# The product of W_v and T: both halves of T in one 256-column matmul, taken from two PSUM banks

## The chip, the cores and the metric

The kernel runs on one core of a Trainium2 chip. The metric is device time in microseconds (us), the median of several runs. The engines are named as the profile names them: PE is TensorE (matmuls; PEld is its weight load), DVE is VectorE, ACT is ScalarE, POOL is GpSimd, SP issues most DMAs.

## The reference, cut to what matters

One transformer block on x of 2048 tokens by 512 features, all in fp32: an adaptive layer norm, linear attention with 32 heads of 16 features, then a bilinear gated unit.

```python
h = layernorm(x) * (1 + ca) + sa
q, k, v = split(h @ wqkv)                            # 512 columns each
pq, pk = phi(q), phi(k)                              # phi(t) = (t+1 if t>0 else exp(t)) + 1e-6
kv  = einsum("bhsd,bhse->bhde", pk, v)               # 16 x 16 per head
den = einsum("bhqd,bhd->bhq", pq, pk.sum(s)) + 1e-6
x = x + ga * ((einsum("bhqd,bhde->bhqe", pq, kv) / den) @ wo)
h = layernorm(x) * (1 + cb) + sb
x = x + gb * (((h @ w_gate) * (h @ w_up)) @ w_down)
```

## The kernel before, in words

Every fp32 operand X of a matmul is held as two tiles of a rounded type, a high part Xh (X copied to that type, on ACT) and a low part Xl = X − Xh (on DVE). A product of two such pairs is three matmuls that add up in PSUM: ah·bh, ah·bl, al·bh. `product` (L215–221) does this with a moving operand of 512 columns.

No v is ever computed for the tokens. A loop over the 16 tiles of 128 tokens adds up T = x̂ᵀ·phi(k), 512 by 512, in the four accumulators `tacc[k]` (`t_tile`), while it projects k of later tiles. After the loop T is scaled by 1 + ca, gets sa times the sum over phi(k) (`zb`), and is split in high and low (`tt_high`, `tt_low`, L780–787). Then `kv_part` (L789–796) multiplies W_vᵀ by T. Only the four 128 by 128 blocks on the diagonal are wanted, since heads of 16 features do not reach beyond them: for each 128-row slice k of W_v and T, and each block g, three matmuls of 128 columns go to the columns g·128 to g·128+127 of one PSUM bank, `kvps`. That makes 4 · 4 · 3 = 48 matmuls.

The bank is then multiplied by the 0/1 mask of the heads (L818, DVE) into `kvf`, and split (L820: ACT L206 for the high part, DVE L207 for the low). `w_full` (L764–772) multiplies each block of the pair `kvp` by a slice of wo and DVE scales the result by ga (L770): this is the folded output weight, which `y_step` applies to phi(q) of each token tile.

The code is in the order in which instructions are issued; no scheduler moves them. Each engine works through its own instructions in that order and waits by semaphore for the others. Around the change, q of tiles 6 to 11 is projected between the steps: `proj` is twelve matmuls of 512 columns (L219, L220, L221, four times) into a bank of the pool `ps_w`; `q_a` is two ACT instructions on it (L327, L328); `q_b` is one DVE instruction (L331) that reads the bank for the last time. `ps_w` has four banks and `ps_acc` four; a new bank waits for the last reader of the tile that held it. `den_a` is DVE work on the denominators (L712, L718). The piece in question runs, in the program's order: projection 7; `kv_part(0, 1)`; `q_b(6)`, `q_b(7)`; projection 8; `den_a`; `kv_part(2, 3)`; mask and split; `q_a(8)`; projection 9; `q_b(8)`; `w_out(0, 1)`, which is `w_full` and a split; `q_b(9)`; projection 10; `w_full(2, 3)`; projection 11.

The line numbers above are those of the kernel before. In the changed kernel the halves of T are split on L792 and L796, the matmuls are L805 and L806, and the result is taken on L812 to L815.

Of the kernel before, what the change touches and what calls it, by code (L numbers as in the profile page):

```python
# [9 lines left out]
F32R = mybir.dt.float32r  # L10
AF = mybir.ActivationFunctionType
ALU = mybir.AluOpType
AX = mybir.AxisListType

P = 128
# [7 lines left out]
def tile_adaln_block(  # L23
# [12 lines left out]
    nc = tc.nc  # L36
    ctx.enter_context(tc.manual_schedule())
    _, S, D = x.shape
    F = w_gate.shape[1]
    KD = D // P  # L40
# [21 lines left out]
    ps_acc = pool("ps_acc", 4, space=bass.MemoryType.PSUM)  # L62
    ps_w = pool("ps_w", 4, space=bass.MemoryType.PSUM)

    def f32(ap):
        return ap.bitcast(F32)
# [3 lines left out]
    def T(p, tag, shape=(P, D), dt=F32, bufs=None):  # L70
        cnt[0] += 1
        return p.tile(list(shape), dt, tag="t" if p is tiles else tag, name=f"{tag}_{cnt[0]}", bufs=bufs)

    def B(tag, shape=(P, D), dt=F32):

        return T(tiles, tag, shape, dt)

    def acc_bank():
        return T(ps_acc, "acc")

    def bank():
        return T(ps_w, "bank")
# [7 lines left out]
    mask = consts.tile([P, P], F32, name="mask")  # L90
# [114 lines left out]
    def split(src, h, l, low=None):  # L205
        nc.scalar.activation(h, src, AF.Copy)  # L206
        (low or nc.vector).tensor_tensor(l, src, f32(h), op=ALU.subtract)  # L207
# [7 lines left out]
    def product(ps, pairs, begin=True, end=True):  # L215

        n = len(pairs)
        for i, ((ah, al), (bh, bl)) in enumerate(pairs):
            nc.tensor.matmul(ps, ah, bh, start=begin and i == 0, stop=False)  # L219
            nc.tensor.matmul(ps, ah, bl, start=False, stop=False)  # L220
            nc.tensor.matmul(ps, al, bh, start=False, stop=end and i == n - 1)  # L221
# [13 lines left out]
    def cut(pair, a, b):  # L235
        return pair[0][:, a:b], pair[1][:, a:b]
# [78 lines left out]
    wk, wq, wv = [], [], []  # L315
    kx, phk, phq, q_ps = {}, {}, {}, {}

    def proj(i, w, of=bank):

        ch, j = divmod(i, NJ)  # L320
        ps = of()
        product(ps, [(cut(norm[ch].t[k], j * P, (j + 1) * P), w[k]) for k in range(KD)])
        return ps
# [52 lines left out]
    def q_a(i, ps):  # L376
        phq[i] = B("h")
        q_ps[i] = ps
        phi_a(ps, phq[i])

    def q_b(i):
        phi_b(q_ps.pop(i), phq[i])
# [193 lines left out]
    raw_m, raw_o, wo_s = {}, [], []  # L576
# [143 lines left out]
    def den_a(ch, *js, on=None):  # L720

        for j in js:
            den_p(ch, j, on=on)
            den_r(ch, j)
# [25 lines left out]
    def q_tile(i):  # L750
        q_a(i, proj(i, wq))
# [3 lines left out]
    def w_out(*gs):  # L755
        fs = w_full(*gs)
        for f in fs:
            w_split(f)
# [5 lines left out]
    def w_full(*gs):  # L764
        fs = []
        for g in gs:
            ps = bank()
            product(ps, [(cut(kvp, g * P, (g + 1) * P), wo_s[g])])
            f = B("n")
            nc.vector.tensor_tensor(f, ps, ga, op=ALU.mult)  # L770
            fs.append(f)
        return fs
# [4 lines left out]
    ps = proj(6, wq)  # L777
    fs, tt = [], []

    def tt_high(k):  # L780
        f = fs[k]
        nc.vector.scalar_tensor_tensor(f, zb, sa[:, k:k + 1], f, op0=ALU.mult, op1=ALU.add)
        tt.append((B("w", dt=F32R), B("w", dt=F32R)))
        nc.scalar.activation(tt[k][0], f, AF.Copy)

    def tt_low(k):
        nc.vector.tensor_tensor(tt[k][1], fs[k], f32(tt[k][0]), op=ALU.subtract)

    def kv_part(*ks):  # L789
        for k in ks:  # L790
            for g in range(KD):
                a, b = g * P, (g + 1) * P  # L792
                (ah, al), (bh, bl) = cut(wv[k], a, b), cut(tt[k], a, b)
                for n, (x, y) in enumerate(((ah, bh), (ah, bl), (al, bh))):
                    nc.tensor.matmul(kvps[:, a:b], x, y, start=k + g + n == 0, stop=k == KD - 1 and n == 2,
                                     skip_group_check=True)  # L796

    for k in range(KD):
        fs.append(B("n"))
# [1 line left out]
    for k in range(KD):  # L801
        tt_high(k)
        if k:
            tt_low(k - 1)
    tt_low(KD - 1)  # L805
    q_a(6, ps)  # L806
    q_tile(7)
    kvps = acc_bank()
    kv_part(0, 1)
    q_b(6)  # L810
    q_b(7)
    den_p(1, 2)  # L812
    ps = proj(8, wq)
    den_a(0, 2, 3, on=nc.vector)
    kv_part(2, 3)  # L815
    kvp = (B("xh", dt=F32R), B("xl", dt=F32R))
    kvf = B("n")
    nc.vector.tensor_tensor(kvf.rearrange("p (g c) -> p g c", g=KD), kvps.rearrange("p (g c) -> p g c", g=KD),  # L818
                            mask.unsqueeze(1).to_broadcast([P, KD, P]), op=ALU.mult)
    split(kvf, *kvp)  # L820
    q_a(8, ps)
    ps = proj(9, wq)
    q_b(8)
# [4 lines left out]
    ps = proj(10, wq)  # L828
    den_c(0)
    q_a(10, ps)  # L830
    wf = w_full(2, 3)
    den_c(1)
    ps = bank()
# [607 lines left out]
    for n, (s, g, f) in enumerate(order):  # L1441
        groups = groups_of[s]
        first, final = f == groups[g][0], f == groups[g][-1]
# [8 lines left out]
        at = {p: list(early.get((n, p), ())) for p in ("a11", "s1", "s2", "s3", "mid", "s4", "pe")}  # L1452
# [39 lines left out]
        if (s, f) in pair_of:  # L1492
            at_first = f == groups[g][0]
            p = pairs.setdefault((s, g), Pair())
# [20 lines left out]
        if was and was[:2] in paired and was[2] == groups_of[was[0]][was[1]][1]:  # L1515
            of, p = was[0], pairs[was[:2]]
# [87 lines left out]
```

## Time and profile before

| | |
|---|---|
| median of 3 runs | 553.78 us (553.54, 553.78, 557.78) |
| span of the profiled execution, first to last instruction | 552.4 us |
| median less the span | 1.4 us |
| mean granted TensorE clock | 0.999 |
| PE busy | 545.8 us (99%) |
| DVE busy | 432.2 us (78%); 26.07 of 28 us from 152 to 180 us |
| ACT busy | 299.5 us (54%) |
| POOL busy | 176.8 us (32%) |
| the 48 matmuls of L795 | 132.7 to 141.2 us of the span, in two pieces of 24 |

Times within the span are counted from its first instruction. A row of the timeline gives the start, how long it took, engine, line, what it wrote and read with the shape of its tile, and in brackets how long the engine had been idle and what ended that. Instructions of one engine overlap at their ends, so the distance from one start to the next is shorter than a duration; where the two differ, the text says which is meant.

### The profile page before, as it was taken

Reading aid. Unit: us, or ns where it says so; the run is one execution under the profiler, and the core shown is the slowest. Engines: PE = TensorE matmul, PEld = TensorE weight load, DVE = VectorE, ACT = ScalarE, POOL = GpSimd, SP = SyncE. Lnnn points to the kernel's source line nnn. Section 1 sums busy time; section 2 is a strip of 40 time slices with the busy share of each in tenths; the row PEclk is TensorE's granted clock in tenths of the full one; section 3 lists DMA queues with packets and bytes.
Section 4 is the critical chain, followed back from the end, with each engine's and each line's share of the span. In section 5 each row is a group of like instructions: output and inputs, shape, how many; then the busy total and the mean of one; then the engine's idle time right before and its main releaser. Section 6 shows DMA issues by size and latency. Waiting matters only on the chain. (4 is left out here: it accounts for less than half of the span.)

```text
span 552.4 us, 8146 instructions
## 1 busy us (share of the span) xinstructions
PE 545.8 (99%) x2775; PEld 460.1 (83%) x2775; DVE 432.2 (78%) x794; ACT 299.5 (54%) x535; POOL 176.8 (32%) x180
## 2 busy tenths in 40 slices
PE   8999999999999999999999999999999999999997
PEld 6888888888888888888888888878888888888886
DVE  6878779978998998865655767797577877879696
ACT  4876857456467876654545355463243534453540
POOL 2000000003527646353556644540002524242400
PEclk9999999999999999999999999999999999999999
DMA  8910224203230045195888634289786534342004
GB/s 256 373 57 1 76 77 152 77 0 77 78 115 2 0 154 189 39 316 180 285 286 274 222 123 163 87 312 391 231 259 218 173 131 138 129 146 86 1 0 153
DMA packets 58512, 83.24 MB, mean 151 GB/s; under 512 B 6564, under 2 KB 23720, under 8 KB 58472
## 3 DMA queue, kind: packets, MB, share of 16 engines
q1 hardware_dynamic: 56544, 81.16, 44.1%
q10 hardware_dynamic: 1928, 1.58, 0.9%
q8 instruction: 22, 0.36, 0.3%
q14 instruction: 18, 0.15, 0.1%
HBM read 53.02 MB, written 29.69 MB: 150 GB/s over the span
## 5 line engine op out<-in xcount | busy, mean ns | idle before, releaser
L1057 PE MATMUL bank<-h,w 128*128 128x512 f32 (+1 forms) x924 | 221.6, 391 | 0.2 <-POOL w L1020 0.2
L1057 PEld LDWEIGHTS bank<-h,w 128*128 128x128 f32 (+1 forms) x924 | 168.2, 186 | 36.2 <-POOL w L1020 0.6
L1063 ACT ACTIVATE bank<-bank 128x512 f32<-128x512 f32 (+2 forms) x46 | 26.2, 571 | 122.7 <-PE bank L1057 122.5
L1253 DVE TENSOR_TENSOR x<-acc,x 128x256 f32<-128x256 f32 x132 | 48.0, 414 | 13.7 <-PE acc L1226 13.1
L1226 PE MATMUL acc<-w,kh 128*128 128x256 f32 x308 | 57.1, 282 | 0.0
L1226 PEld LDWEIGHTS acc<-w,kh 128*128 128x128 f32 x308 | 50.6, 190 | 3.7
L1020 POOL TENSOR_TENSOR w<-raw,w 128x256 fp32r<-128x256 f32 (+3 forms) x22 | 24.7, 1121 | 73.7 <-ACT w L1013 64.1
L219 PE MATMUL bank<-w,h 128*128 128x512 f32 x112 | 44.1, 394 | 0.0
L221 PE MATMUL bank<-w,h 128*128 128x512 f32 x112 | 43.7, 390 | 0.0
L220 PE MATMUL bank<-w,h 128*128 128x512 f32 x112 | 43.6, 390 | 0.0
L1226 PE MATMUL acc<-w,kl 128*128 128x256 f32 x154 | 43.5, 283 | 0.0
L871 PE MATMUL acc<-w,xh 128*128 128x512 f32 x128 | 40.7, 399 | 0.0
L712 POOL TENSOR_TENSOR f<-h,zb 128x512 f32<-128x512 f32 x12 | 17.5, 1468 | 62.9 <-ACT zb L692 48.9
L262 POOL TENSOR_TENSOR rstd<-ve,half 128x4 f32<-128x4 f32 (+3 forms) x12 | 11.2, 935 | 81.4 <-DVE ve L259 68.0
L1083 DVE TENSOR_TENSOR phi<-bank,g 128x512 f32<-128x512 f32 (+1 forms) x22 | 15.1, 687 | 25.2 <-PE bank L1057 25.2
L1063 ACT ACTIVATE u<-bank 128x512 f32<-128x512 f32 (+1 forms) x44 | 26.1, 594 | 15.4 <-PE bank L1057 15.2
L1113 DVE TENSOR_TENSOR g<-bank,u 128x512 f32<-128x512 f32 (+1 forms) x22 | 15.2, 689 | 21.2 <-ACT u L1063 19.9
L1020 POOL TENSOR_TENSOR w<-t,w 128x512 fp32r<-128x512 f32 (+1 forms) x22 | 29.6, 1346 | 0.0
L1146 PE MATMUL acc<-w,kh 128*128 128x512 f32 (+1 forms) x76 | 29.6, 390 | 0.0
L1147 PE MATMUL acc<-w,kh 128*128 128x512 f32 (+1 forms) x76 | 29.6, 390 | 0.0
L1148 PE MATMUL acc<-w,kl 128*128 128x512 f32 (+1 forms) x76 | 29.6, 389 | 0.0
L277 ACT ACTIVATE n<-x,nmr,rstd 128x512 f32<-128x512 f32 x31 | 23.6, 808 | 10.9 <-DVE nmr L267 10.7
(204 smaller groups left out, 1187.0 us busy)
## 6 DMA issues: line engine op xcount, KB each, us to landing
right<-w SPq DMA_DIRECT2D x56, 256.0 KB, 3.7
w<-right SPq DMA_DIRECT2D x56, 256.0 KB, 4.3
x<-in_A_x_dram SPq DMA_DIRECT2D x22, 256.0 KB, 5.2
raw<-in_w_mod_dram SPq DMA_DIRECT2D x22, 256.0 KB, 3.7
raw<-in_B_w_down_dram SPq DMA_DIRECT2D x18, 256.0 KB, 3.0
side_s<-h SPq DMA_DIRECT2D x16, 256.0 KB, 2.6
h<-side_s SPq DMA_DIRECT2D x16, 256.0 KB, 5.3
raw<-in_A_wqkv_dram SPq DMA_DIRECT2D x12, 256.0 KB, 6.2
```

The source lines that it names most:

```text
L219: nc.tensor.matmul(ps, ah, bh, start=begin and i == 0, stop=False)
L220: nc.tensor.matmul(ps, ah, bl, start=False, stop=False)
L221: nc.tensor.matmul(ps, al, bh, start=False, stop=end and i == n - 1)
L871: nc.tensor.matmul(yps[i], x, y, start=fresh and k + n == 0, stop=k == KD - 1 and n == 2, skip_group_check=True)
L1020: sub = lambda out, x, y: (on or nc.gpsimd).tensor_tensor(out, x, f32(y), op=ALU.subtract)
L1057: mm = lambda x, y, **kw: nc.tensor.matmul(ps, x[:, k], y, skip_group_check=True, **kw)
L1063: nc.scalar.activation(out, x, AF.Copy)
L1146: nc.tensor.matmul(dn[j], hh[:n, a:b], dh[:n], start=i == 0, stop=False)
L1147: nc.tensor.matmul(dn[j], hh[:n, a:b], dl[:n], start=False, stop=False)
L1148: nc.tensor.matmul(dn[j], hl[:n, a:b], dh[:n], start=False, stop=i == n_of - 1)
L1226: mm = lambda x, y, **kw: nc.tensor.matmul(ps, x[:, a:b], y, skip_group_check=True, **kw)
L1253: nc.vector.tensor_tensor(xt[:, halves[at]], banks[b][m], xt[:, halves[at]], op=ALU.add)
```

## The change

The high and low part of T now lie side by side: for each k there are two tiles (one for blocks 0 and 1, one for blocks 2 and 3, called s below), each laid out as block, part, column. One matmul of 256 columns multiplies W_v's high part by both parts of T at once and leaves the two results side by side; a second one of 128 columns adds W_v's low part times T's high part to the second of them. The results of s = 0 and s = 1 are in two PSUM banks. The second call is ordered by s: all of s = 0, then all of s = 1. Each bank is taken by itself: ACT copies the second result to SBUF, DVE adds the first, DVE multiplies by the mask, and the split follows, each on 256 columns.

```diff
     def tt_high(k):
         f = fs[k]
         nc.vector.scalar_tensor_tensor(f, zb, sa[:, k:k + 1], f, op0=ALU.mult, op1=ALU.add)
-        tt.append((B("w", dt=F32R), B("w", dt=F32R)))
-        nc.scalar.activation(tt[k][0], f, AF.Copy)
+        tt.append([B("w", (P, KG, 2, P), F32R) for _ in range(2)])
+        for s in range(2):
+            nc.scalar.activation(tt[k][s][:, :, 0], pairs_of(f)[:, s], AF.Copy)
 
     def tt_low(k):
-        nc.vector.tensor_tensor(tt[k][1], fs[k], f32(tt[k][0]), op=ALU.subtract)
+        for s in range(2):
+            nc.vector.tensor_tensor(tt[k][s][:, :, 1], pairs_of(fs[k])[:, s], f32(tt[k][s])[:, :, 0], op=ALU.subtract)
 
-    def kv_part(*ks):
+    def kv_part(s, *ks):
         for k in ks:
-            for g in range(KD):
-                a, b = g * P, (g + 1) * P
-                (ah, al), (bh, bl) = cut(wv[k], a, b), cut(tt[k], a, b)
-                for n, (x, y) in enumerate(((ah, bh), (ah, bl), (al, bh))):
-                    nc.tensor.matmul(kvps[:, a:b], x, y, start=k + g + n == 0, stop=k == KD - 1 and n == 2,
-                                     skip_group_check=True)
+            for g in range(KG):
+                a = (s * KG + g) * P
+                (ah, al), both_b = cut(wv[k], a, a + P), tt[k][s][:, g]
+                first, last = k + g == 0, k == KD - 1
+                nc.tensor.matmul(kvps[s][:, g], ah, both_b, start=first, stop=False, skip_group_check=True)
+                nc.tensor.matmul(kvps[s][:, g, 1], al, both_b[:, 0], start=False, stop=last, skip_group_check=True)
+
+    kvp = [(B("xh", (P, KG, P), F32R), B("xl", (P, KG, P), F32R)) for _ in range(2)]
+
+    def kv_take(s):
+        low, f = B("n", (P, KG, P)), B("n", (P, KG, P))
+        nc.scalar.activation(low, kvps[s][:, :, 1], AF.Copy)
+        nc.vector.tensor_tensor(f, kvps[s][:, :, 0], low, op=ALU.add)
+        nc.vector.tensor_tensor(f, f, mask.unsqueeze(1).to_broadcast([P, KG, P]), op=ALU.mult)
+        split(f, *kvp[s])
...
-    kvps = acc_bank()
-    kv_part(0, 1)
+    kvps = [T(ps_acc, "acc", (P, KG, 2, P)) for _ in range(2)]
+    for k in range(2):
+        for s in range(2):
+            kv_part(s, k)
     q_b(6)
     q_b(7)
     den_p(1, 2)
     ps = proj(8, wq)
     den_a(0, 2, 3, on=nc.vector)
-    kv_part(2, 3)
-    kvp = (B("xh", dt=F32R), B("xl", dt=F32R))
-    kvf = B("n")
-    nc.vector.tensor_tensor(kvf.rearrange("p (g c) -> p g c", g=KD), kvps.rearrange("p (g c) -> p g c", g=KD),
-                            mask.unsqueeze(1).to_broadcast([P, KD, P]), op=ALU.mult)
-    split(kvf, *kvp)
+    for s in range(2):
+        kv_part(s, 2, 3)
+        kv_take(s)
     q_a(8, ps)
     ps = proj(9, wq)
     q_b(8)
```

Here `KG` is 2, and `pairs_of` views a 512-column tile as half s, block g, column.

Three places show what this makes of the instructions. On PE, at the end of projection 7 and the start of the first piece, before; a row gives line, operation, what it writes, the moving and the stationary operand, and the shape written (`acc` is the PSUM bank, w_1455 and w_1456 the high and low part of T, w_783 and w_784 those of W_v):

```order
L219 MATMUL bank_1477<-w_418,h_611 128x512
L220 MATMUL bank_1477<-w_419,h_611 128x512
L221 MATMUL bank_1477<-w_418,h_612 128x512
L795 MATMUL acc_1493<-w_1455,w_783 128x128
L795 MATMUL acc_1493<-w_1456,w_783 128x128
L795 MATMUL acc_1493<-w_1455,w_784 128x128
```

The same place on PE in the changed kernel (acc_1505 is the bank of s = 0, w_1459 the tile with both parts of T's blocks 0 and 1):

```order
L219 MATMUL bank_1489<-w_418,h_611 128x512
L220 MATMUL bank_1489<-w_419,h_611 128x512
L221 MATMUL bank_1489<-w_418,h_612 128x512
L805 MATMUL acc_1505<-w_1459,w_783 128x256
L806 MATMUL acc_1505<-w_1459,w_784 128x128
```

Three matmuls of 128 columns became one of 256 and one of 128; the projections stand where they stood. The second piece, behind projection 8, has all of bank acc_1505 first and then all of acc_1506. On ACT, from the phi of q tile 7 (h_1490) to that of tile 8 (h_1571), before:

```order
L327 ACTIVATE h_1490<-bank_1477 128x512
L328 ACTIVATE h_1490<-h_1490 128x512
L206 ACTIVATE xh_1565<-n_1567 128x512
L327 ACTIVATE h_1571<-bank_1522 128x512
L328 ACTIVATE h_1571<-h_1571 128x512
```

The same place on ACT in the changed kernel, where h_1502 is tile 7 and h_1576 tile 8:

```order
L327 ACTIVATE h_1502<-bank_1489 128x512
L328 ACTIVATE h_1502<-h_1502 128x512
L812 ACTIVATE n_1554<-acc_1505 128x256
L206 ACTIVATE xh_1446<-n_1555 128x256
L812 ACTIVATE n_1569<-acc_1506 128x256
L206 ACTIVATE xh_1448<-n_1570 128x256
L327 ACTIVATE h_1576<-bank_1527 128x512
```

One instruction between the two tiles became four, which alternate between the two halves. On DVE, from the end of `den_a` to `q_b(8)`, before:

```order
L718 TENSOR_REDUCE den_1428<-f_1538 128x32
L818 TENSOR_TENSOR n_1567<-acc_1493,mask 128x512
L207 TENSOR_TENSOR xl_1566<-n_1567,xh_1565 128x512
L331 SCALAR_TENSOR_TENSOR h_1571<-bank_1522,h_1571 128x512
L727 TENSOR_TENSOR den_1428<-den_1428,den_1419 128x128
```

The same place on DVE in the changed kernel:

```order
L718 TENSOR_REDUCE den_1428<-f_1543 128x32
L813 TENSOR_TENSOR n_1555<-acc_1505,n_1554 128x256
L814 TENSOR_TENSOR n_1555<-n_1555,mask 128x256
L207 TENSOR_TENSOR xl_1447<-n_1555,xh_1446 128x256
L813 TENSOR_TENSOR n_1570<-acc_1506,n_1569 128x256
L814 TENSOR_TENSOR n_1570<-n_1570,mask 128x256
L207 TENSOR_TENSOR xl_1449<-n_1570,xh_1448 128x256
L331 SCALAR_TENSOR_TENSOR h_1576<-bank_1527,h_1576 128x512
```

Two instructions of 512 columns became six of 256, and `q_b(8)` stands behind all six.

More of the change, by code (lines that the diff above doesn't have):

```diff
@@ L767, in w_full @@
             ps = bank()
-            product(ps, [(cut(kvp, g * P, (g + 1) * P), wo_s[g])])
+            (h, l), at = kvp[g // KG], g % KG
+            product(ps, [((h[:, at], l[:, at]), wo_s[g])])
             f = B("n")
@@ L778, in tile_adaln_block, with pairs_of @@
     fs, tt = [], []
+    KG = KD // 2
+    def pairs_of(x):
+        return x.rearrange("p (s g c) -> p s g c", s=2, g=KG)
     def tt_high(k):
```

## The prediction

> **What bounds the kernel now.** I read the page first, its shares of busy time.
>
> ```profile
> PE 545.8 (99%) x2775; PEld 460.1 (83%) x2775; DVE 432.2 (78%) x794; ACT 299.5 (54%) x535; POOL 176.8 (32%) x180
> ```
>
> PE is never idle to speak of, so the second view is its waits, over the whole span:
>
> ```profile
> PE acc L153 <- DVE w L148: 2.0, 1, 2.0
> PE bank L295 <- ACT n L277: 0.6, 1, 0.6
> PE bank L1057 <- POOL w L1020: 0.2, 1, 0.2
> ```
>
> These are all of them, us in total, times, longest. None lies between 118 and 180 us, the stretch around the change. So there a microsecond less on PE is a microsecond less in the span, as long as nothing else comes late; and a wait newly made on PE costs its full length. How near the other engines are to being late is the question, and the timeline answers it. PE through the change:
>
> ```profile
> 132.94 2.79 PE L795 MATMUL acc<-w,w 128*128 128x128 f32 x24
> 135.57 0.45 PE L219 MATMUL bank<-w,h 128*128 128x512 f32 x1
> ...
> 138.40 2.79 PE L795 MATMUL acc<-w,w 128*128 128x128 f32 x24
> 141.03 0.45 PE L219 MATMUL bank<-w,h 128*128 128x512 f32 x1
> ...
> 143.86 0.39 PE L219 MATMUL bank<-w,xh 128*128 128x512 f32 x1
> ...
> 145.22 0.39 PE L219 MATMUL bank<-w,h 128*128 128x512 f32 x1
> ...
> 149.30 0.39 PE L219 MATMUL bank<-w,h 128*128 128x512 f32 x1
> ```
>
> In order: first piece of the product, projection 8 (135.57), second piece, projection 9 (141.03), `w_full(0, 1)` (143.86), projection 10 (145.22), and, six matmuls of `w_full(2, 3)` later, projection 11 (149.30). DVE and ACT at the same time:
>
> ```profile
> 132.89 0.68 DVE L787 TENSOR_TENSOR w<-n,w 128x512 fp32r<-128x512 f32 x1
> ...
> 134.15 1.47 DVE L787 TENSOR_TENSOR w<-n,w 128x512 fp32r<-128x512 f32 x2
> ...
> 137.23 0.69 DVE L331 SCALAR_TENSOR_TENSOR h<-bank,h 128x512 f32<-128x512 f32 x1 [0.46 <-ACT h L328]
> 137.84 0.91 DVE L712 TENSOR_TENSOR f<-h,zb 128x512 f32<-128x512 f32 x1
> 138.79 0.69 DVE L718 TENSOR_REDUCE den<-f 128x32 f32<-128x512 f32 x1
> 139.39 1.06 DVE L712 TENSOR_TENSOR f<-h,zb 128x512 f32<-128x512 f32 x1
> 140.48 0.69 DVE L718 TENSOR_REDUCE den<-f 128x32 f32<-128x512 f32 x1
> 141.23 0.69 DVE L818 TENSOR_TENSOR n<-acc,mask 128x512 f32<-128x512 f32 x1
> 142.62 1.19 DVE L207 TENSOR_TENSOR xl<-n,xh 128x512 fp32r<-128x512 f32 x1 [0.70 <-ACT xh L206]
> 143.77 0.69 DVE L331 SCALAR_TENSOR_TENSOR h<-bank,h 128x512 f32<-128x512 f32 x1
> ...
> 148.10 0.68 DVE L331 SCALAR_TENSOR_TENSOR h<-bank,h 128x512 f32<-128x512 f32 x1
> ```
>
> ```profile
> 134.27 0.63 ACT L784 ACTIVATE w<-n 128x512 fp32r<-128x512 f32 x1 [0.63 <-DVE n L782]
> 134.81 0.58 ACT L327 ACTIVATE h<-bank 128x512 f32<-128x512 f32 x1
> ...
> 141.95 0.63 ACT L206 ACTIVATE xh<-n 128x512 fp32r<-128x512 f32 x1 [4.75 <-DVE n L818]
> 142.49 0.58 ACT L327 ACTIVATE h<-bank 128x512 f32<-128x512 f32 x1
> 143.10 0.63 ACT L328 ACTIVATE h<-h 128x512 f32<-128x512 f32 x1
> ```
>
> DVE works without a pause from 137.23 to 141.17, until the end of `den_a`. The last L795 starts at 141.03 − 0.11 = 140.92 and the mask at 141.23, so PE and DVE arrive at the mask together. From there runs a chain over DVE and ACT: mask, L206, L327, L328, and L331 at 143.77, which is `q_b(8)`. It ends at 143.77 + 0.69 = 144.46. That frees the bank which projection 10 takes at 145.22. **PE has 0.76 us in hand there.** Next, `q_b(9)` at 148.10 ends at 148.78 and frees the bank of projection 11 (149.30): 0.52 us in hand. A gain on PE larger than these is lost to these two waits unless DVE comes earlier by as much.
>
> **The change, part by part.** *The matmuls.* 24 of them take 135.57 − 132.94 = 2.63 us from start to start, 0.110 each. A 256-column matmul of this kernel, among its like:
>
> ```profile
> 442.13 0.40 PE L1226 MATMUL acc<-w,kh 128*128 128x256 f32 x2
> 442.37 0.28 PE L1226 MATMUL acc<-w,kl 128*128 128x256 f32 x1
> 442.49 0.40 PE L1226 MATMUL acc<-w,kh 128*128 128x256 f32 x2
> ```
>
> Three in 0.36 us, 0.120 each. Each of the 16 triples of 0.329 becomes 0.120 + 0.110 = 0.230. The product costs 3.67 us instead of 5.26: **PE saves 1.59 us**, 0.79 in each piece, and would reach projection 9 at 139.44, `w_full` at 142.27 and projection 10 at 143.63.
>
> The Trainium skill ("TensorE: Matmul & The Clock Gate", Back-to-back issue gap) gives an isolated spacing of columns / 2.4 plus 2.5 ns. By that rule one matmul of 256 columns (109 ns) costs as much as two of 128 (56 ns each), and the estimate of the saving is 0.04 us. The rows disagree at 128 columns: 110 ns here, about twice that figure; the measurement decides.
>
> *The split of T.* Four copies on ACT and four subtractions on DVE become eight of each, of half the width. Rows of 256 columns:
>
> ```profile
> L1253 DVE TENSOR_TENSOR x<-acc,x 128x256 f32<-128x256 f32 x132 | 48.0, 414 | 13.7 <-PE acc L1226 13.1
> L1013 ACT ACTIVATE w<-raw 128x256 fp32r<-128x256 f32 x10 | 4.3, 429 | 0.0
> ...
> 440.28 1.41 DVE L1253 TENSOR_TENSOR x<-acc,x 128x256 f32<-128x256 f32 x4
> ```
>
> On DVE 0.41 us, and (1.41 − 0.41) / 3 = 0.33 from start to start, against 0.60 for 512 columns (137.23 to 137.84). Eight times 0.33 less four times 0.60 is 0.24 us more. But a subtraction can start after half a copy, and ACT has 0.63 us idle before its last copy. I let `q_a(6)`, `q_b(6)`, `q_b(7)` and `den_a` end 0.1 us later (0 to 0.25): at 141.27. PE reads T's slice 1 at 132.94 + 0.92 = 133.86 instead of 134.26. DVE makes its low part from 132.89 on; in two halves that is done by 133.3 and 133.7. That is close and costs at most 0.2 us, which the wait below would swallow. Slices 2 and 3 (from 134.15) are read by the second piece alone.
>
> *Taking the result.* This is the part that decides. Before there were mask and split, 512 wide; now the program's order gives DVE add, mask, low, add, mask, low, and ACT copy, high, copy, high, and only then `q_a(8)`. The first bank is full at about 138.5 and its ACT copy is early, hidden behind `den_a`. But DVE only takes the add after `den_a`; the second copy stands on ACT behind the first high part, which waits for the first mask; so both halves run one behind the other. With 0.41 per DVE step, 0.42 per ACT step and 0.03 for a hand-over (140.48 + 0.69 to 141.23 includes one; 141.92 to 141.95 another):
>
> - first add starts 0.60 after the L718 (140.48) plus the 0.1: 141.18; ends 141.59
> - first mask 141.62 to 142.03; first high part on ACT 142.06 to 142.48
> - first low part on DVE 142.51 to 142.92; beside it the second copy on ACT, done at 142.8
> - second add 142.84 to 143.25; second mask 143.28 to 143.69; second high part 143.72 to 144.14
> - L327 starts 0.31 to 0.33 after that high part did: 144.05 (before 142.49)
> - `q_b(8)` is 1.28 behind L327 (142.49 to 143.77): 145.33, ends 146.02 (before 144.46)
>
> So `q_b(8)` comes 1.56 us later, where PE wants the bank 1.59 us earlier. Projection 10 starts at 146.06 instead of 145.22. `w_full(0, 1)` is ready to start at 142.27 but its high part comes at 142.5 and its low part at 142.9: a first wait of some 0.3 us, which is inside the second. From `q_b(8)` to `q_b(9)` DVE and ACT have their own chain of 148.10 − 143.77 = 4.33 us, with nothing idle over 0.1: `q_b(9)` starts at 149.66 and ends at 150.34, and projection 11 starts at 150.38 instead of 149.30. That is **1.1 us later**, with no allowance yet for POOL.
>
> *POOL beside it.* POOL adds up weights at that time:
>
> ```profile
> 139.86 1.18 POOL L1002 TENSOR_TENSOR t<-raw 128x256 f32<-128x256 f32 x1
> ...
> 142.52 0.74 POOL L1002 TENSOR_TENSOR t<-raw,t 128x256 f32<-128x256 f32 x1
> ```
>
> The L207 at 142.62, which meets the last of these, took 1.19 us instead of 0.69; the L818 at 141.23 and the L718 at 140.48, beside others, took 0.69. The old mask read PSUM; the new mask reads two SBUF tiles, as L207 does. The first mask, the first low part and the second mask may each be held up, by 0 to 0.37 (half of 0.74). The Trainium skill says the same ("SBUF — State Buffer", Who interferes with whom): a DVE instruction with two SBUF inputs contends with a POOL instruction that reads SBUF, one with a single SBUF input does not; 1.19 against 0.69 us agrees. Since the L207 lies in the middle of such a stretch I take 0.4 in all (0 to 1.1). Projection 11 is then 1.5 us late.
>
> *What follows.* PE runs without a wait behind 149.30, and DVE, whose share there is 26.07 of 28 us, is moved by as much as PE, so nothing is caught up:
>
> ```profile
> 152.00:180.00 28.00, 28.00 (x141) 22.95 (x140) 26.07 (x52) 20.70 (x39) 14.35 (x15) 1.00 0.20 57
> ```
>
> Columns: PE, PEld, DVE, ACT, POOL busy. The DMAs of SP keep their order, and the five more SBUF tiles that the change takes from a pool of 99 I cost at nothing; the loads they could hold back are wanted by POOL, for which PE waited 0.2 us in all.
>
> **The sum.** 552.4 of span plus 1.5 is 553.9; the median of the runs is 1.4 above the span, so **555.3 us**. Bounds: halves at half the price of wholes (0.35 on both engines instead of 0.41 and 0.42, seven steps in the chain) and no meeting with POOL, +0.7; all delays by POOL at their upper end and 0.4 in hand-overs, +2.6. That is 554.5 to 556.4.
>
> **Rivals.** *A, the saving stays*: 553.78 − 1.59 = 552.2 us. It needs `q_b(8)` to end by 143.6, before the time that it has now, so the six DVE steps would have to be no longer than the two. Each row of 256 columns speaks against it; for it speaks only that the first half is ready 2.7 us before DVE takes it. In between, with a chain some 1 us shorter than I think, lies no change, 553.5 to 554.4. By the Trainium skill's rule for the spacing (the section named above) even A would give 553.7. *B, halves cost like wholes* (0.69 and 0.63, the fixed part of an instruction rules): the eight subtractions take 8 · 0.60 − 4 · 0.60 = 2.4 us more ahead of `den_a`, of which 0.2 is hidden, and the chain from the add to the second high part 4.9 instead of 3.0, plus 0.2 before L327. Together with the 1.1 that is 2.1 + 1.9 + 0.2 + 1.1 = 5.3 late, 559.1 us, and with POOL's 0.4, 559.5. It passes 1% from about 0.68 us per half on DVE. The rows with 0.41 and 0.42 speak against it; that T's halves are written with gaps of 128 columns, a form with no row before, speaks for it a little. *C, the 256-column matmul costs two of 128*: PE saves nothing, wants projection 10 at 145.22 and still gets its bank at 146.06 or later. The end is the forecast's, 555.3; only the product's 5.26 us would tell.
>
> **Chances.** Forecast (with C) 0.78; A 0.06; in between 0.10; B 0.04; anything else slower 0.02. The range reaches from A's 552.2 to the forecast's upper bound and a little run-to-run difference, 556.8. About 1% of 553.8, 5.5 us, is what a measurement of this kernel can tell from no change. None but B passes it: faster 0.02, same 0.93, slower 0.05.
>
> **What would show it.** L805 and L806 together 3.7 us (5.26: C). PE waiting for DVE's `q_b` line L331 at projection 10, about 2.0 to 2.7 us, after up to 0.5 at `w_full` for L206; projection 11 1.1 to 1.5 us later than 149.30, and the same shift at the end of the span. DVE's L796 at 0.41 us; one of L814 and the first L207 above 0.5 us. I am wrong if PE has no wait at projection 10, if the shift is not kept to the end, or if a wait for a DMA or a weight of POOL appears that is not there now.

## The result, and the profile after

The changed kernel takes **557.92 us** (median of 5 runs, 556.49 to 558.08) against 554.20 us for the kernel before in the same comparison (median of 5): a ratio of 1.0058, 95% interval 1.0037 to 1.0079. The medians lie 3.7 us apart. That is inside the 1% that I called "same", though the interval, 0.4 to 0.8% above the kernel before, shows that a difference well under 1% can be told here. It is 2.6 us above the predicted 555.3 and 1.1 above the upper end of the range, 556.8.

First the view of waits of the changed kernel, PE only, from 130 to 156 us (us in total, times, longest). Before there was none here:

```profile
PE bank L219 <- DVE h L331: 2.0, 1, 2.0
PE bank L219 <- ACT xh L206: 0.5, 1, 0.5
```

These are the two waits of the prediction: `w_full(0, 1)` for the high part, then projection 10 for `q_b(8)`. The timeline of PE in the changed kernel, with the first row of each stretch:

```profile
132.93 0.28 PE L805 MATMUL acc<-w,w 128*128 128x256 f32 x1
...
134.72 0.45 PE L219 MATMUL bank<-w,h 128*128 128x512 f32 x1
...
137.53 0.28 PE L805 MATMUL acc<-w,w 128*128 128x256 f32 x1
...
139.32 0.45 PE L219 MATMUL bank<-w,h 128*128 128x512 f32 x1
...
142.74 0.50 PE L219 MATMUL bank<-w,xh 128*128 128x512 f32 x1 [0.46 <-ACT xh L206]
...
146.40 0.50 PE L219 MATMUL bank<-w,h 128*128 128x512 f32 x1 [1.99 <-DVE h L331]
...
147.94 0.63 PE L221 MATMUL bank<-w,h 128*128 128x512 f32 x1
148.36 0.63 PE L219 MATMUL bank<-w,h 128*128 128x512 f32 x1
148.79 0.63 PE L220 MATMUL bank<-w,h 128*128 128x512 f32 x1
...
152.25 0.39 PE L219 MATMUL bank<-w,h 128*128 128x512 f32 x1
152.47 0.40 PE L220 MATMUL bank<-w,h 128*128 128x512 f32 x1
152.71 0.39 PE L221 MATMUL bank<-w,h 128*128 128x512 f32 x1
```

The two pieces of the product cost 1.79 us each (132.93 to 134.72, 137.53 to 139.32), 3.58 in all instead of 5.26. Projection 10 starts at 146.40, 1.18 us later than before. So far everything is as forecast. But between there and projection 11 (152.25) the matmuls stand 0.43 us apart (147.94, 148.36, 148.79) where 0.23 is usual (152.25, 152.47, 152.71), and projection 11 comes 2.95 us late, not 1.1 to 1.5. The view by stretches shows why. Columns: length, busy time of PE, PEld, DVE, ACT and POOL with instructions in brackets, granted clock of PE, DMA share, GB/s:

```profile
140.51:143.92 3.41, 2.95 (x13) 2.05 (x12) 2.82 (x7) 0.69 (x2) 3.16 (x4) 1.00 0.00 0
143.92:147.33 3.41, 1.42 (x7) 0.85 (x6) 2.17 (x5) 2.65 (x5) 0.90 (x1) 1.00 0.48 157
147.33:150.75 3.42, 3.42 (x10) 2.63 (x9) 3.32 (x7) 1.23 (x2) 0.39 (x1) 0.50 0.52 152
150.75:154.16 3.41, 3.41 (x18) 2.80 (x18) 2.93 (x5) 1.87 (x3) 1.62 (x1) 1.00 0.00 0
```

From 147.33 to 150.75 us **PE was granted half its clock**. The 3.41 us before that hold the whole wait of 1.99 us: PE was busy for 1.42 of them. The prediction has no word on this.

From projection 11 on the shift is kept: the last matmul ends at 551.45 us (548.50 before), 2.95 later. The span is longer by 3.7 (556.1 against 552.4); the other 0.8 lies behind the last matmul and is taken up below.

### The profile page after: what moved, and what is told of

Same layout as the page of the kernel before. It is cut to its first block, busy times and chain, and to the rows that moved or that the text cites. A ratio compares the mean times of both kernels' runs of the same rounds, so it can differ in the third digit from the quotient of the medians.

```text
span 556.1 us, 8131 instructions
## 1 busy us (share of the span) xinstructions
PE 546.7 (98%) x2759; PEld 459.6 (83%) x2759; DVE 433.6 (78%) x802; ACT 300.5 (54%) x542; POOL 177.2 (32%) x180
## 5 line engine op out<-in xcount | busy, mean ns | idle before, releaser
L219 PE MATMUL bank<-w,h 128*128 128x512 f32 x112 | 44.8, 400 | 2.0 <-DVE h L331 2.0
L220 PE MATMUL bank<-w,h 128*128 128x512 f32 x112 | 44.4, 396 | 0.0
L221 PE MATMUL bank<-w,h 128*128 128x512 f32 x112 | 44.3, 395 | 0.0
L712 POOL TENSOR_TENSOR f<-h,zb 128x512 f32<-128x512 f32 x12 | 17.5, 1468 | 64.4 <-ACT zb L692 48.8
L1244 PEld LDWEIGHTS acc<-w,kl 128*128 128x128 f32 x154 | 29.3, 191 | 0.0
```

Of the source, the lines that this page charges most:

```text
L1244: mm = lambda x, y, **kw: nc.tensor.matmul(ps, x[:, a:b], y, skip_group_check=True, **kw)
```

## The experiments

The median of the kernel before was 554.49, 554.03 and 554.20 us (17, 23 and 9 runs) in the three groups of runs below, and each time is compared with the one of its group.

**The two kernels again (e7_before2, e8_after2, e11_after3).** No edit.

> The kernel before, unchanged, for a second profile. It tells how much the time from the end of the last matmul to the end of the span, 3.89 us in the first profile, differs from run to run: after the change it was 4.66, and 4.4 to 5.0 in the runs so far. If it is 3.9 again, the change or its neighbours lengthen the end of the program by 0.5 us and more; if it is 4.4 or more, the first profile was a lucky one, and 0.77 us of the difference between the two first profiles is no effect of the change.

> The changed kernel, unchanged, for a second profile. The two waits of PE, 0.46 and 1.99 us, and the start of projection 10 near 146.4 us should come again. The half-clock stretch should follow them again if the idle time is always long enough, and lie at the same place behind projection 10's start within 1 us if it is set off by the wait alone; if its start differs by more, something that runs freely decides too. The time from the last matmul to the end: 4.4 to 4.8 us.

> The changed kernel again, beside the two others: 557.7 us, with a mean clock of .994 to .997 in most runs; a run with a mean clock of .999 or 1.000 lies at 556.0 to 556.6.

The kernel before: 554.94 us (one run), span 553.2, no wait around the change. The changed kernel in e8: 557.72 us (one run), waits of 0.5 and 2.0 again, half clock from 146.65 to 150.06. That stretch begins 0.31 us behind the start of projection 10 (146.34) and began 0.93 behind it in the first profile, less than 1 us apart, so by the measure that I had set e8 alone does not show that something runs freely; e11 does. In e11: 556.81 us as a median, but its four runs are 557.37 and 557.26 at a mean clock of .994 and .995, and 556.36 and 556.20 at 1.000 and .998 (I had expected the low clock in most). The profile is of the last one, and it has the same two waits:

```profile
PE bank L219 <- DVE h L331: 2.0, 1, 2.0
PE bank L219 <- ACT xh L206: 0.5, 1, 0.5
```

```profile
142.16:145.58 3.42, 2.12 (x8) 1.00 (x7) 2.11 (x5) 1.84 (x5) 1.92 (x3) 1.00 0.10 36
145.58:148.99 3.41, 2.26 (x10) 1.90 (x11) 2.97 (x5) 2.04 (x4) 1.30 (x1) 1.00 0.70 195
148.99:152.40 3.41, 3.41 (x16) 2.53 (x15) 3.31 (x7) 2.07 (x5) 1.25 (x1) 1.00 0.21 79
```

The clock is whole. So the same program with the same waits is halved in one run and not in another. Over the ten runs of the changed kernel, seven lie at 557.2 to 558.1 with a mean clock of .994 to .997, three at 556.2 to 556.5 with .998 to 1.000. The difference, 557.7 − 556.4, is 1.3 us; half of 3.42 would be 1.7. A low mean clock alone does not prove this wait, though: one of the 49 runs of the kernel before in the three groups has .994 too (557.98 us), and so has one of the eleven of e2 (558.11 us). The profiles of these two kernels, taken of other runs, have no wait of 2 us around the change. What lowered the clock in the two runs is not known.

What decides between halved and whole in the changed kernel, as far as the profiles show, is where the wait falls on a grid in time: in these profiles the clock changes only at points of such a grid. In the first profile it is halved at 147.33, whole at 150.75 and, after the last matmul, halved for good at 553.52, by the same view:

```profile
550.11:553.52 3.41, 1.34 (x12) 1.14 (x10) 1.51 (x4) 0.00 (x0) 0.00 (x0) 1.00 0.72 236
553.52:556.10 2.58, 0.00 (x0) 0.00 (x0) 0.00 (x0) 0.00 (x0) 0.00 (x0) 0.50 0.05 16
```

553.52 − 150.75 = 402.77 us is 118 stretches of 3.413. e11 has its last change at 551.76:

```profile
551.76:554.50 2.74, 0.00 (x0) 0.00 (x0) 0.00 (x0) 0.00 (x0) 0.00 (x0) 0.50 0.14 49
```

118, 119 and 120 stretches before that are 148.99, 145.58 and 142.16, the bounds of the rows above. There the wait of 2.0 us (144.73 to 146.73) is cut in two by the bound at 145.58, and no stretch has less than 2.12 us of PE work. In the two halved profiles the grid puts all of the wait in one stretch (143.92 to 147.33; in e8 143.23 to 146.65). If the grid fell at random, a wait of 2.0 us would lie wholly in one stretch in some four runs of ten, (3.41 − 2.0) / 3.41, which is an estimate; seven of ten is more than that, but ten runs are too few to tell. For the seven runs without a profile only the mean clock is on record.

**Spare matmuls in the waits (e1_fill, e9_fill4, e10_fill2).** The changed kernel with matmuls whose result nobody reads, in the places where PE waits; e1 has 2 and 8, e9 0 and 4, e10 2 and 0.

```diff
     q_a(9, ps)
+    spare = acc_bank()
+    def fill(n):
+        for _ in range(n):
+            nc.tensor.matmul(spare, norm[2].t[0][0][:, :P], wq[0][0], start=True, stop=True)
+    fill(2)
     w_out(0, 1)
+    fill(8)
     q_b(9)
     ps = proj(10, wq)
```

> The changed kernel with ten more matmuls of 512 columns on PE, into a PSUM bank that nobody reads: two in front of w_full(0, 1), eight behind it, where PE waits 0.46 and 1.99 us. The waits themselves stay: projection 10 still starts when q_b(8) has ended, near 146.4 us. Theory (PE's idling is what halves the granted clock from 147.33 to 150.75 us): no half-clock stretch, granted clock 1.000, projection 11 at about 150.7 instead of 152.25 us, and a time 1.5 us below the changed kernel, about 556.4. Rival (the half-clock stretch has another cause and lies there by chance): it is still there, and the time stays near 557.9.

> The changed kernel with four spare matmuls (0.92 us at whole clock) behind w_full(0, 1) and none ahead of it, so that PE waits 0.46 us for the high part and about 1.1 us for q_b(8), 1.5 us in all instead of 2.45. Projection 10 starts where it did, at 146.4. Theory 'a sum of waits sets the clock off, and 1.5 us is too little': no stretch of half clock, projection 11 at 150.7, time 556.1 us as with ten spare matmuls. Rival 'any wait of a microsecond does it': half clock for 3.4 us, 557.7 us.

> The changed kernel with two spare matmuls ahead of w_full(0, 1) and none behind, so that the first wait goes (0.46 us) and the second stays (2.0 us). Theory 'the sum of both waits, 2.45 us, is just enough': whole clock in most runs, 556.1 us. Rival 'the one wait of 2.0 us is what does it': half clock as in the changed kernel, 557.7 us and a mean clock of .995.

| | waits of PE, us | median, us | ratio to before, 95% interval | lowest mean clock of a run |
|---|---|---|---|---|
| changed kernel | 0.5 + 2.0 | 557.92 | 1.0037 to 1.0079 | .994 |
| e1: 2 and 8 spare | 0.2 | 556.06 | 1.0022 to 1.0044 | .998 |
| e9: 0 and 4 spare | 0.4 + 1.1 | 555.62 | 1.0020 to 1.0046 | .998 |
| e10: 2 and 0 spare | 2.0 | 556.28 | 1.0022 to 1.0048 | .995 |

Matmuls that add nothing to the result make the kernel faster: e1 by 1.9 us against the first result, e9 and e10 by 1.2 and 0.5 against e11, which ran beside them. The intervals overlap with those of the changed kernel, and the 0.5 of e10 is not clear of the noise. The single runs of e1 and e9 tell more: nine of the eleven lie at 555.6 to 556.2 us, where the changed kernel has one run of ten. The two others (557.62 and 557.11) took longer at a mean clock of .998 and .999, so the clock is not what sets them apart, and no profile shows what does. In e1 projection 10 starts at 146.38, where it did without them (146.40), and projection 11 at 150.71 instead of 152.25, by PE's timeline of e1:

```profile
146.38 0.50 PE L219 MATMUL bank<-w,h 128*128 128x512 f32 x1 [0.19 <-DVE h L331]
...
150.71 0.50 PE L219 MATMUL bank<-w,h 128*128 128x512 f32 x1
```

The shift there is 150.71 − 149.30 = 1.41 us: the size the prediction gave for the waits. The other 1.54 us is the clock, shown by filling idle time and nothing else. It is less than 1.71, half of the halved stretch, because with whole clock PE would have come to projection 11 at 150.54 and waited for `q_b(9)`, which ends at 150.68.

In the five runs of e9 waits of 0.4 and 1.1 us did no harm to the clock (its time is 0.5 us below what I expected). e10 was to tell whether the sum of two waits counts or the long one alone, and its outcome is neither: its profile has the wait of 2.0 us and a whole clock (the grid, bound at 145.60, cuts the wait of 144.49 to 146.49 into 1.11 and 0.89), and one of its five runs has a mean clock of .995 and 557.08 us. The first wait is not needed, as the stretch of 143.92 to 147.33 shows, where it is not inside; but the wait of 2.0 us alone does it in some runs only.

**The saving without the new way of taking the result (e2_saving).** The kernel before, without the product of W_v's high part and T's low part: 32 matmuls instead of 48, mask and split as they were.

```diff
-                for n, (x, y) in enumerate(((ah, bh), (ah, bl), (al, bh))):
-                    nc.tensor.matmul(kvps[:, a:b], x, y, start=k + g + n == 0, stop=k == KD - 1 and n == 2,
+                for n, (x, y) in enumerate(((ah, bh), (al, bh))):
+                    nc.tensor.matmul(kvps[:, a:b], x, y, start=k + g + n == 0, stop=k == KD - 1 and n == 1,
```

> The kernel before with 32 instead of 48 matmuls in the product of W_v and T: the product of W_v's high part with T's low part is left out, nothing else is changed. It is the saving on PE alone (16 times 0.110 = 1.75 us), with the old way of taking the result. Theory (DVE and ACT set the starts of projections 10 and 11 as soon as PE is early): q_b(8) still ends near 144.5 us, projection 10 starts there (0.7 earlier than before) after a wait of about 1.0 us, projection 11 at 148.8 (0.5 earlier), and the time is 0.5 us below the kernel before, 553.7. Rival (a microsecond on PE is a microsecond of time): 1.75 below, 552.4.

555.54 us, 1.0022 (1.0010 to 1.0034). Projections 10 and 11 start where the slack of the prediction puts them (145.22 and 149.30 before), by PE's timeline of e2:

```profile
144.49 0.50 PE L219 MATMUL bank<-w,h 128*128 128x512 f32 x1
...
148.82 0.50 PE L219 MATMUL bank<-w,h 128*128 128x512 f32 x1
```

So of some 1.7 us that PE saves, 0.48 is left at projection 11, and 0.40 at the last matmul, with the result taken as before. The rest goes to `q_b(8)` and `q_b(9)`, which don't move. So the place of the loss is as expected, but the time is not: it rose by 1.05 us where I expected 0.5 less. The end of the span lies 5.0 us behind the last matmul (3.9 and 4.55 in the two profiles of the kernel before) and the time outside the span is 2.3 to 2.4 us instead of 1.8. I have no cause for these two.

**q_a(8) ahead of the product's end (e3_qearly).** One line moved in the changed kernel.

```diff
     den_a(0, 2, 3, on=nc.vector)
+    q_a(8, ps)
     for s in range(2):
         kv_part(s, 2, 3)
         kv_take(s)
-    q_a(8, ps)
     ps = proj(9, wq)
```

> The changed kernel with one line moved: q_a(8) stands ahead of the second piece of the product and of the taking of its result, so that ACT does it from about 137.6 us, while it is idle. Theory (q_a(8) behind the second high part is a good part of the wait): q_b(8) follows the second low part at once, 144.9 instead of 145.66, projection 10 starts at 145.6 instead of 146.40, projection 11 at about 149.9 if the clock stays whole, 1.5 us later if it is halved again; 554.8 or 556.5 us. Rival (the six DVE steps alone make the wait): projection 10 stays at 146.4, and the time at 556.4 to 557.9.

556.30 us, 1.0039 (1.0024 to 1.0054). Counted from the last L718 of `den_a`, `q_b(8)` starts 4.28 us later (141.27 to 145.55) instead of 5.08 (140.58 to 145.66): the 0.8 that L327 and L328 had cost behind the second high part. But in this profile DVE was 0.70 us late already before the split of T, ahead of the moved line (an L718 at 130.25 instead of 129.55). So `q_b(8)` itself came only 0.11 earlier, projection 10 started at 146.28 and projection 11 at 150.61, and the expected 145.6, 149.9 and 554.8 us were missed. The waits are 0.88 and 1.20 us. The stretch of 142.66 to 146.08 holds most of both, 1.76 us of idle time, and the clock stays whole:

```profile
142.66:146.08 3.42, 1.65 (x6) 0.98 (x6) 2.42 (x6) 1.98 (x5) 1.78 (x2) 1.00 0.14 47
```

One of its six runs has .996 and 558.14 us.

**The halves woven (e4_woven).** Both adds, both masks and the first low part ahead of `q_b(8)`, the second behind it; `q_a(8)` early as in e3.

```diff
+    q_a(8, ps)
...
     for s in range(2):
         kv_part(s, 2, 3)
-        kv_take(s)
-    q_a(8, ps)
+        nc.scalar.activation(low[s], kvps[s][:, :, 1], AF.Copy)
+    for s in range(2):
+        nc.vector.tensor_tensor(f[s], kvps[s][:, :, 0], low[s], op=ALU.add)
+    for s in range(2):
+        nc.vector.tensor_tensor(f[s], f[s], mask.unsqueeze(1).to_broadcast([P, KG, P]), op=ALU.mult)
+        nc.scalar.activation(kvp[s][0], f[s], AF.Copy)
+    nc.vector.tensor_tensor(kvp[0][1], f[0], f32(kvp[0][0]), op=ALU.subtract)
     ps = proj(9, wq)
     q_b(8)
+    nc.vector.tensor_tensor(kvp[1][1], f[1], f32(kvp[1][0]), op=ALU.subtract)
```

> The changed kernel with the same instructions in another order: q_a(8) ahead of the second piece; both copies on ACT at once; on DVE add, add, mask, mask, first low part, q_b(8), second low part; so neither engine waits for the other half's step. Theory (the order of taking, not its work, makes the waits): w_full starts near 142.7, projection 10 near 144.2 us without a wait worth naming, projection 11 near 148.5, granted clock 1.000, and a time 0.4 to 0.9 us below the kernel before, 553.3 to 553.8. Rival (the 0.8 us or so of added DVE work is lost in any order, since DVE is busy 26 of 28 us behind it): PE gets to projection 11 early, waits later in the steps up to 180 us, and the time is that of the kernel before, 554.2, or more.

556.21 us, 1.0036 (1.0024 to 1.0048): a miss. `q_b(8)` did come early, but what DVE won it lost beside POOL, by the timelines of DVE and POOL in e4:

```profile
142.07 1.29 DVE L844 TENSOR_TENSOR n<-n,mask 128x256 f32<-128x256 f32 x2
143.28 0.95 DVE L846 TENSOR_TENSOR xl<-n,xh 128x256 fp32r<-128x256 f32 x1
144.15 0.68 DVE L331 SCALAR_TENSOR_TENSOR h<-bank,h 128x512 f32<-128x512 f32 x1
...
145.09 1.38 DVE L727 TENSOR_TENSOR den<-den,den 128x128 f32<-128x128 f32 x1
```

```profile
144.96 1.36 POOL L712 TENSOR_TENSOR f<-h,zb 128x512 f32<-128x512 f32 x1 [1.01 <-ACT h L328]
```

L727 took 0.28 us in the changed kernel and 1.38 here, where POOL's L712 runs from 144.96 to 146.32. `q_b(9)` came no earlier, and PE waited 0.87 us for it at projection 11 (150.65).

**POOL's sums out of the way (e5_apart, e6_poollate).** e5 is e4 with both low parts ahead of `q_b(8)` and with POOL's additions of weights, which ran beside the taking of the result, moved two steps later. e6 does the second alone to the kernel before. The diff is the part that both share.

```diff
-    y_step(0, after=[lambda: q_b(11), lambda: den_q(7), lambda: den_t(4), lambda: right_sums(0)])
+    y_step(0, after=[lambda: q_b(11), lambda: den_q(7), lambda: den_t(4)])
     y_step(1, after=[lambda: den_t(5), lambda: den_q(8)])
-    y_step(2, after=[lambda: den_t(6), lambda: den_q(9), lambda: right_split(0)])
+    y_step(2, after=[lambda: den_t(6), lambda: den_q(9), lambda: right_sums(0), lambda: right_split(0)])
```

> The woven kernel with two more moves: the second low part stands ahead of q_b(8), so that the first step of den_b (L727) follows q_b(8) at once, before POOL's next L712, which q_b(8) releases; and POOL's four additions of right_sums(0) come after den_q(9), 10 us later, so that the masks and low parts have no POOL beside them. Theory (in the woven kernel POOL took back what the order gave: 0.55 us each on the masks and the first low part, 1.1 us on L727): masks 0.75 us for two, low parts 0.42 each, L727 0.28; projection 10 near 144.1 and projection 11 near 148.5 us, 0.8 us before that of the kernel before; last matmul 0.4 to 0.8 us earlier than there; time 553.7 to 554.1 against 554.5 of the kernel before. Rival (DVE's own work, not POOL, makes q_b(9) late): L727 and masks get shorter, but projection 11 stays later than 149.3 us and the time above 554.5.

> The kernel before with one move only: POOL's right_sums(0) after den_q(9), as in the run e5_apart. PE has no wait there in the kernel before, so a freer DVE gives nothing: 554.5, within 0.3 us. If it alone is faster by 0.5 us or more, the gain of e5_apart is not one of the product.

e5: **554.15 us**, ratio 0.9997 (0.9984 to 1.0009), 3.6 us less than the changed kernel beside it (e8, one run). The same DVE steps in e5's timeline:

```profile
141.90 0.75 DVE L844 TENSOR_TENSOR n<-n,mask 128x256 f32<-128x256 f32 x2
142.79 0.76 DVE L847 TENSOR_TENSOR xl<-n,xh 128x256 fp32r<-128x256 f32 x2
143.47 0.68 DVE L331 SCALAR_TENSOR_TENSOR h<-bank,h 128x512 f32<-128x512 f32 x1
```

Two masks cost 0.75 us here and 1.29 in e4. `q_b(8)` starts at 143.47, earlier than in the kernel before (143.77), the wait of 2.0 us is gone and only one of 0.5 at `w_full` is left. Projection 11 starts at 148.53 (0.77 earlier than before the change), and the last matmul ends 1.17 us earlier. Yet the time is that of the kernel before, 554.03 in this group. About 0.5 of the 1.17 is not the product's: the first profile of the kernel before loses it at 361 us, where PE waits for a weight of POOL (the L1057 among the prediction's waits), and the second profile of the kernel before, e5 and e6 do not have that wait. Of the rest, the end of the program takes some: the end of the span lies 4.6 us behind the last matmul in e5, and 3.9 and 4.55 in the two profiles of the kernel before. The time outside the span is 2.0 us on average instead of 1.8.

e6: 554.55 us, 1.0003 (0.9990 to 1.0015), so moving POOL's work is worth nothing without the change. Against e6, which has POOL's work in the same place, e5's last matmul ends 0.64 us earlier, its span is 0.4 shorter (552.0 against 552.4) and its median 0.40 lower, with intervals that overlap. So the best version that I found does no better than the kernel before beyond the noise.

## Why the prediction was right about the place and wrong about the price

**The matmuls.** Forecast 3.67 us for the product, measured 3.58: a saving of 1.68 us. Rival C (a 256-column matmul costs two of 128) falls.

**The split of T.** Forecast 0.1 us late; the last L718 of `den_a` starts at 140.58, where it started at 140.48 in the kernel before. The last four of the eight L796 take 1.43 us together and 0.42 us one by one, so rival B (halves cost like wholes) falls:

```profile
134.14 1.43 DVE L796 TENSOR_TENSOR w<-n,w 128x256 fp32r<-128x256 f32 x4
```

**Taking the result.** The steps one by one, on DVE and then on ACT in the changed kernel:

```profile
140.58 0.69 DVE L718 TENSOR_REDUCE den<-f 128x32 f32<-128x512 f32 x1
141.18 0.41 DVE L813 TENSOR_TENSOR n<-acc,n 128x256 f32<-128x256 f32 x1
141.63 0.61 DVE L814 TENSOR_TENSOR n<-n,mask 128x256 f32<-128x256 f32 x1
142.72 0.42 DVE L207 TENSOR_TENSOR xl<-n,xh 128x256 fp32r<-128x256 f32 x1 [0.48 <-ACT xh L206]
143.07 0.42 DVE L813 TENSOR_TENSOR n<-acc,n 128x256 f32<-128x256 f32 x1
143.52 0.51 DVE L814 TENSOR_TENSOR n<-n,mask 128x256 f32<-128x256 f32 x1
144.51 0.43 DVE L207 TENSOR_TENSOR xl<-n,xh 128x256 fp32r<-128x256 f32 x1 [0.48 <-ACT xh L206]
145.66 0.69 DVE L331 SCALAR_TENSOR_TENSOR h<-bank,h 128x512 f32<-128x512 f32 x1 [0.72 <-ACT h L328]
...
149.99 0.69 DVE L331 SCALAR_TENSOR_TENSOR h<-bank,h 128x512 f32<-128x512 f32 x1
```

```profile
144.06 0.42 ACT L206 ACTIVATE xh<-n 128x256 fp32r<-128x256 f32 x1 [1.10 <-DVE n L814]
144.39 0.58 ACT L327 ACTIVATE h<-bank 128x512 f32<-128x512 f32 x1
```

Forecast: first add 141.18, first high part 142.06, second high part 143.72, L327 144.05, `q_b(8)` 145.33, with 0.4 for POOL 145.73. Measured: 141.18, 142.28, 144.06, 144.39, 145.66. POOL cost 0.2 at the first mask (0.61 against 0.41) and 0.1 at the second: 0.3 of the 0.4 allowed. Rival A (the saving stays) falls, and e2 shows that even with the old chain only 0.48 us of the saving is left at projection 11.

**The wait on PE.** Forecast 2.0 to 2.7 us after up to 0.5; measured 1.99 after 0.46. `q_b(9)` follows at 149.99, 4.33 us behind `q_b(8)` as forecast, and with whole clock projection 11 starts at 150.71 (e1), 1.41 late; forecast 1.1, with POOL 1.5. The two listed waits, 2.45 us, cost PE 2.89 from start to start: projection 9 began 1.71 early and projection 10 1.18 late. A listed wait counts from the end of the last matmul (144.01 + 0.40), and the next one would have started 0.23 behind that one's start.

**What follows: here it failed.** The step that failed is "a wait newly made on PE costs its full length": the sum has the waits and no term for what the clock does behind them. In the first profile the second wait left PE busy for only 1.42 of the 3.41 us of a stretch, the next stretch ran at half clock, and this cost 1.54 us more at projection 11. By the mean clock it happened in 7 of 10 runs, so the median carries it. "Nothing is caught up" held: the 2.95 us at projection 11 are 2.95 at the last matmul. "I am wrong if …" does not name the clock: none of its three conditions came about.

**The sum.** 557.92 − 555.3 = 2.62 us is made up of +1.54 (the clock), −0.09 (projection 11 at 1.41 instead of 1.5 with the clock whole), +0.77 (last matmul to the end of the span: 4.66 us against 3.89) and +0.4 (time outside the span: 1.8 us, where I took 1.4 from a median and a span of different runs). The last two have nothing to do with the change that I could find: the distance behind the last matmul is 4.55 us in the second profile of the kernel before and between 3.9 and 5.0 in all profiles here, so 3.89 was a low one. I worked from one profile and gave no width to either. The three runs with whole clock, 556.2 to 556.5, lie within the range, about one us above the forecast, which is the size of these two items.

The rival "slower" was tied to the price of a half on DVE (0.68 us). The real one needed no dearer instruction.

## What to carry to other kernels

A wait on PE can have a second price. Here a wait that left PE busy for 1.42 of the 3.41 us between two points of the clock's grid was followed by half clock up to the next point, and 2.0 us of wait cost 1.5 more, in some runs and not in others. When a forecast has PE waiting for about 2 us within so short a time, in a kernel that hardly waits, look at the granted clock by stretches, and give the range that price; 1.76 us of idle time in one stretch, the nearest case below, was followed by whole clock (e3). And a saving on the engine that bounds the kernel is worth only what the next buffer's release has in hand: count that slack first (here 0.5 to 0.8 us against a saving of 1.7).

## What the runs showed of the hardware

- **The clock changes on a grid of 3.413 us that does not start with the kernel.** It has a point at 147.33 in the first profile, at 146.65 in e8 and at 145.58 in e11. The first profile has whole clock from 150.75 to 553.52, 118 periods; the halved stretch lasts 3.42 us there and 3.41 in e8. The Trainium skill ("TensorE: Matmul & The Clock Gate", What's actually happening) gives a free-running window of 3413 ns; these traces agree to the third digit.
- **A window need not be empty to be followed by half clock.** The same page of the Trainium skill asks for at least one idle window (and in "Why this matters for your kernels" for gaps of over about 3 us). Here a gap of 1.99 us was enough, in a window with PE busy for 1.42 of 3.41 us (1.41 in e8); windows with 1.65 (e3) and 2.12 us (e11) were followed by whole clock. Busy time is not the whole measure, though: at the end of e10 a window with 1.77 us of matmuls of 256 columns, nine of the fifteen 96 rows high, was followed by half clock (the rows below), and at the end of e8 one with 1.93 us by whole clock (549.42 to 552.83). How the activity is weighed was not tried.

```profile
548.37:551.78 3.41, 1.77 (x15) 1.56 (x14) 1.94 (x6) 0.00 (x0) 0.00 (x0) 1.00 0.71 233
551.78:554.50 2.72, 0.00 (x0) 0.00 (x0) 0.00 (x0) 0.00 (x0) 0.00 (x0) 0.50 0.23 75
```

- **A short DVE instruction can be held up for almost the length of the POOL instruction beside it.** L727 (128 columns, both inputs in SBUF) went from 0.28 to 1.38 us in e4 beside a POOL instruction of 1.36 us. My bound for such a meeting was half of a POOL instruction. In three such meetings the one that started first kept its time: POOL at 144.96 against L727 at 145.09; in the kernel before POOL at 142.52 (0.74 us) against L207 at 142.62 (1.19); and in e2, where L207 is the first, DVE keeps its 0.69 and POOL takes 1.24 instead of 0.74:

```profile
142.59 0.69 DVE L207 TENSOR_TENSOR xl<-n,xh 128x512 fp32r<-128x512 f32 x1 [0.70 <-ACT xh L206]
```

```profile
142.64 1.24 POOL L1002 TENSOR_TENSOR t<-raw,t 128x256 f32<-128x256 f32 x1
```
